# A fused attention and gated feed-forward kernel: batch 0 from a hand-written list, its bounds as pair tiles in two passes, two queues in written order, preparation shared differently between ACT and DVE

## The chip, the cores and the metric

The kernel runs on one core of one Trainium2 chip. Its engines are TensorE (PE), VectorE (DVE), ScalarE (ACT) and GpSimd (POOL); SyncE (SP) issues most of the DMA. The metric is the device time of one execution in microseconds (us), and where a kernel ran several times the median is quoted. The kernel before took 366.93 us (median of 3 runs, 365.98 to 369.07).

## The reference, cut to what matters

```python
# q, k, v: 4 batches x 8 heads x 768 rows x 64, fp32;  x: 3072 tokens x 512;  d_ff 1536
k_min, k_max = per chunk of 32 keys                      # 24 chunks
ub  = sum_d max(q * k_min, q * k_max)                    # upper bound of q.k in a chunk
ub  = where(causal by chunk, ub, -1e9)
sel = the 6 chunks with the largest ub, for each query
attn = softmax(where(sel and causal, q k^T / 8, -1e9))
x    = attn @ v, heads side by side
out  = (sigmoid(x @ w_gate) * (x @ w_val)) @ w_out
```

## The kernel before

The work goes in eight units of half a batch: 0a, 0b, 1a, ..., 3b. A unit has 384 queries; an "a" unit holds rows 0 to 383 of a batch, a "b" unit rows 384 to 767. A unit has three parts:

- **Preparation**: keys and queries are transposed on TensorE, two heads (a pair) to a block of PSUM, the memory in which this kernel's matmuls leave their results. From the keys come each chunk's maxima and minima, and an f16 copy `headK`. From the queries come their positive and negative parts (the "signs", `qs`) and an f16 copy `headQ`. A bounds matmul and a pick give 0/1 marks, written as 32 more rows under `headQ`. Under `headK` lies a fixed pattern (`epat`) that turns a mark into a large negative score.
- **Attention**: score matmuls, exp on ACT, a causal select on POOL, value matmuls.
- **FFN**: twelve gate and value blocks and three output blocks.

A loop merges the attention of unit i, the preparation of unit i+1 and the FFN of unit i-1. Inside that loop a scheduler may reorder the instructions of each engine. Only `first_prep` is held as written.

```python
def fill_kept(i, eng):                    # eng: gpsimd, for both buffers
    eng.memset(kcat[i], 0.0)
    eng.memset(v16s[i][:, :, :, D:D + 1], 1.0)
    for h in range(H):
        eng.tensor_copy(headK[i][64:96, h, :], epat)      # pattern under the keys

def keys_t(u, p, pool):                   # p: pair of heads
    ...                                   # 3 transposes into ps, 2 reduces on DVE into u.kmm
def keys_f(u, p, engs):
    ps = u.kps.pop(p)
    for e in range(2):
        engs[e](headK[u.b % 2][0:64, 2 * p + e, u.rows], ps[64 * e:64 * e + 64])

def chunks_t(u):                          # kmax over kmin, one head to 128 rows
    c0 = T // CH * u.half
    for e in range(2):
        for i in range(2):
            nc.scalar.copy(kcat[u.b % 2][64 * i:64 * i + 64, e:H:2, c0:c0 + T // CH],
                           u.kmm[64 * e:64 * e + 64, :, i, :])

def queries_t(u, p, pool):
    ...                                   # 3 transposes into ps
    for e in range(2):
        src = ps[64 * e:64 * e + 64]
        nc.scalar.activation(u.qs[0:64, 2 * p + e, s0:T], src[:, s0:T], AF.Relu)
        nc.vector.tensor_scalar_min(u.qs[64:128, 2 * p + e, s0:T], src[:, s0:T], 0.0)

def ffn_gv(u, fb):                        # one gate and one value block
    gp = pff.tile(...)                    # 4 matmuls
    nc.scalar.activation(gate, gp, AF.Tanh, scale=0.5)
    vp = pff.tile(...)                    # 4 matmuls; pff has 3 buffers
    nc.vector.scalar_tensor_tensor(hg, gate, 1.0, vp, ALU.add, ALU.mult)

SV = (nc.scalar.copy, nc.vector.tensor_copy)
SS = (nc.scalar.copy, nc.scalar.copy)
def prep_tasks(u):                        # for every unit but 0a
    r = [(0.0, lambda: regroup(u, "k", GP)), (0.0, lambda: regroup(u, "q", GP))]
    for p in range(NP):
        r.append((0.4, lambda p=p: (keys_t(u, p, ppr), keys_f(u, p, SV))))
    r.append((0.0, lambda: (chunks_t(u), cast_v(u))))
    for p in range(NP):
        r.append((0.4, lambda p=p: (queries_t(u, p, ppr), queries_f(u, p, SS))))
    ...                                   # bounds, pick, pick_t

load(units[1])
with tc.manual_schedule():                # this part runs as written
    fill_kept(0, nc.gpsimd)
    first_prep(units[0])
load_w(0)
...                                       # the loop that merges; fill_kept(1, nc.gpsimd) at i == 0
```

The softmax here doesn't subtract the row's maximum and nothing guards it: scores larger than these inputs give would overflow.

Of the kernel before, what the change touches and what calls it, by code (L numbers as in the profile page):

```python
# [18 lines left out]
def kernel(  # L19
# [10 lines left out]
    nc = tc.nc  # L30

# [28 lines left out]
    class Unit:  # L60
        def __init__(self, b, half):
            self.b, self.half = b, half
            self.name = f"{b}{'ab'[half]}"
            self.qa, self.qb = HB * half, HB * half + HB
            self.rows = slice(T * half, T * half + T)
            self.sel0 = 1 - half
            self.m = HB - self.sel0
            self.cb = T // CH * (half + 1)
            self.banks = HIGH if half else LOW
            self.where = {}  # L70
            base = 0
            for bk in self.banks:
                for (jb, i0, n) in bk:
                    for o in range(0, n, 128):
                        self.where[((i0 + o) // 128, jb)] = base + o
                    base += n
            self.width = base
            self.att, self.pv, self.kps, self.qps, self.ubT = {}, {}, {}, {}, {}
# [25 lines left out]
    def regroup(u, n, parts):  # L104
# [7 lines left out]
    load(units[0])  # L112

    ident32 = consts.tile([128, 128], F32, tag="id32")
    make_identity(nc, ident32)
    ident16 = consts.tile([128, 128], F16, tag="id16")
    nc.vector.tensor_copy(ident16, ident32)
    epat = consts.tile([32, NC, CH], F16, tag="epat")
    nc.vector.memset(epat, 0.0)
    nc.gpsimd.affine_select(  # L120
        out=epat, in_=epat, compare_op=ALU.not_equal, fill=NEG,
        base=0, pattern=[[-1, NC], [0, CH]], channel_multiplier=1,
    )
    epat = epat.rearrange("p c s -> p (c s)")
    NQ = 2 * HB - 1
    pen = consts.tile([128, NQ, NC], F32, tag="pen")
    nc.vector.memset(pen, 0.0)
    nc.gpsimd.affine_select(
        out=pen, in_=pen, compare_op=ALU.is_ge, fill=-1e9,
        base=128, pattern=[[128, NQ], [-CH, NC]], channel_multiplier=1,  # L130
    )

# [8 lines left out]
    def fill_kept(i, eng):  # L141
        eng.memset(kcat[i], 0.0)
        eng.memset(v16s[i][:, :, :, D:D + 1], 1.0)
        for h in range(H):
            eng.tensor_copy(headK[i][64:96, h, :], epat)  # L145

    nc.vector.memset(apt[0], 0.0)
    nc.vector.memset(apt[1], 0.0)
    nc.vector.memset(headQ[0][64:96, :, 0:128], 0.0)
# [8 lines left out]
    def load_w(i):  # L158
        lo, hi = 512 * i, 512 * i + 512
        tc.keep_in_program_order(nc.gpsimd.dma_start(wg16[:, :, lo:hi], wgs[:, :, lo:hi]))  # L160
        tc.keep_in_program_order(nc.gpsimd.dma_start(wv16[:, :, lo:hi], wvs[:, :, lo:hi]))

    def load_wo(i):
        tc.keep_in_program_order(nc.gpsimd.dma_start(wo16[:, 4 * i:4 * i + 4, :], wos[:, 4 * i:4 * i + 4, :]))
# [4 lines left out]
    def keys_t(u, p, pool):  # L169
        if p == 0:  # L170
            u.kmm = sel.tile([128, NP, 2, T // CH], F32, tag="kmm", name=f"kmm_{u.name}")
        ps = pool.tile([128, T], F32, tag="ps", name=f"kT_{u.name}_{p}")
        for x in range(HB):
            nc.tensor.transpose(ps[:, x:T:HB],  # L174
                                u.k[:, x, 2 * p:2 * p + 2, :].rearrange("p h d -> p (h d)"), ident32)
        pv = ps.rearrange("p (c s) -> p c s", s=CH)
        for e, op in enumerate((ALU.max, ALU.min)):
            nc.vector.tensor_reduce(out=u.kmm[:, p, e, :], in_=pv, op=op, axis=AX.X)  # L178
        u.kps[p] = ps

    def keys_f(u, p, engs):
        ps = u.kps.pop(p)
        for e in range(2):
            engs[e](headK[u.b % 2][0:64, 2 * p + e, u.rows], ps[64 * e:64 * e + 64])  # L184

    def chunks_t(u):
        c0 = T // CH * u.half
        for e in range(2):
            for i in range(2):
                nc.scalar.copy(kcat[u.b % 2][64 * i:64 * i + 64, e:H:2, c0:c0 + T // CH],  # L190
                               u.kmm[64 * e:64 * e + 64, :, i, :])

    def queries_t(u, p, pool):
        if p == 0:
            u.qs = sel.tile([128, H, T], F32, tag="qs", name=f"qs_{u.name}")
        ps = pool.tile([128, T], F32, tag="ps", name=f"qT_{u.name}_{p}")
        for x in range(HB):
            nc.tensor.transpose(ps[:, x:T:HB],  # L198
                                u.q[:, x, 2 * p:2 * p + 2, :].rearrange("p h d -> p (h d)"), ident32)
        s0 = 128 * u.sel0  # L200
        for e in range(2):
            src = ps[64 * e:64 * e + 64]
            nc.scalar.activation(u.qs[0:64, 2 * p + e, s0:T], src[:, s0:T], AF.Relu)
            nc.vector.tensor_scalar_min(u.qs[64:128, 2 * p + e, s0:T], src[:, s0:T], 0.0)
        u.qps[p] = ps

    def queries_f(u, p, engs):
        ps = u.qps.pop(p)
        for e in range(2):
            engs[e](headQ[u.half][0:64, 2 * p + e, :], ps[64 * e:64 * e + 64])  # L210

    def bounds(u, j):
        s0 = 128 * u.sel0
        n = T - s0
        ps = ppr.tile([128, T], F32, tag="ps", name=f"ubT_{u.name}_{j}")
        for i in range(4):
            nc.tensor.matmul(ps[32 * i:32 * i + 32, 0:n], kcat[u.b % 2][:, 4 * j + i, :],  # L217
                             u.qs[:, 4 * j + i, s0:T], start=True, stop=True)
        t = ubp.tile([128, T], F32, tag="ubT", name=f"ubTs_{u.name}_{j}")
        nc.scalar.copy(t[:, 0:n], ps[:, 0:n])  # L220
        u.ubT[j] = t
# [18 lines left out]
    def pick_t(u, j):  # L240
        ps = ppr.tile([128, T], F16, tag="ps", name=f"apT_{u.name}_{j}")
        for x in range(u.sel0, HB):
            nc.tensor.transpose(ps[:, 128 * x:128 * x + 128],  # L243
                                apt[j][:, x, :, :].rearrange("p h c -> p (h c)"), ident16)
        s0 = 128 * u.sel0
        for i in range(4):
            if i % 2 == 0:
                nc.scalar.copy(headQ[u.half][64:96, 4 * j + i, s0:T], ps[32 * i:32 * i + 32, s0:T])  # L248
            else:
                nc.vector.tensor_copy(headQ[u.half][64:96, 4 * j + i, s0:T], ps[32 * i:32 * i + 32, s0:T])  # L250

    def score(u, h, x):
# [5 lines left out]
        ps = psc.tile([128, n], F32, tag="ps", name=f"sc_{u.name}_{h}_{x}")  # L258
# [70 lines left out]
    VS = (nc.vector.tensor_copy, nc.scalar.copy)  # L329
    SV = (nc.scalar.copy, nc.vector.tensor_copy)  # L330
    SS = (nc.scalar.copy, nc.scalar.copy)
    GP = [(nc.gpsimd.tensor_copy, 0, H)]

    def prep_tasks(u):
        r = [(0.0, lambda: regroup(u, "k", GP)), (0.0, lambda: regroup(u, "q", GP))]
        for p in range(NP):
            r.append((0.4, lambda p=p: (keys_t(u, p, ppr), keys_f(u, p, SV))))
        r.append((0.0, lambda: (chunks_t(u), cast_v(u))))
        for p in range(NP):
            r.append((0.4, lambda p=p: (queries_t(u, p, ppr), queries_f(u, p, SS))))  # L340
# [4 lines left out]
        for j in range(2):  # L345
            r.append((0.06 * u.m, lambda j=j: pick_t(u, j)))
        return r

    def first_prep(u):
        A, V, G = nc.scalar.copy, nc.vector.tensor_copy, nc.gpsimd.tensor_copy  # L350
        regroup(u, "k", [(V, 0, 2), (A, 2, 4)])
        regroup(u, "k", [(V, 4, 6), (A, 6, 8)])
        for p in range(NP):
            keys_t(u, p, (ppr, ppr, psc, psc)[p])
            keys_f(u, p, SS)
        regroup(u, "q", [(A, 0, 2), (G, 2, 4), (A, 4, 6), (G, 6, 8)])
        for p in range(NP):
            queries_t(u, p, (psc, ppr, ppr, psc)[p])
            if p == 1:
                chunks_t(u)  # L360
                queries_f(u, 0, SS)
                queries_f(u, 1, SV)
                bounds(u, 0)
        cast_v(u)
        pick(u, 0)
        queries_f(u, 2, SS)
        bounds(u, 1)
        queries_f(u, 3, SS)
        pick_t(u, 0)
        pick(u, 1)  # L370
        pick_t(u, 1)
# [39 lines left out]
    load(units[1])  # L411
    with tc.manual_schedule():
        fill_kept(0, nc.gpsimd)
        first_prep(units[0])
    load_w(0)
    prev = []
    for i, u in enumerate(units):
        prep = []
        if i + 1 < len(units):
            prep = prep_tasks(units[i + 1])  # L420
# [3 lines left out]
        if i == 0:  # L424
            a.append((0.0, lambda: fill_kept(1, nc.gpsimd)))
            for n in range(3):
                a.insert(len(a) * (n + 1) // 4, (0.0, (lambda n=n: load_w(n + 1)) if n < 2 else (
                    lambda: [load_wo(j) for j in range(3)])))
# [34 lines left out]
```

## Time and profile before

| | before |
|---|---|
| time, median | 366.93 us |
| span of the profiled execution | 366.9 us (this run took 368.6, the slow end of the runs) |
| TensorE (PE) busy | 320.4 us, 87% |
| ACT, DVE, POOL busy | 67%, 56%, 24% |
| first score matmul of 0a, 0b, 1a | 19.8, 62.3, 107.6 us (of 0a one ran alone at 19.8; the others begin at 25.3, the figure in the prediction) |

The first lines of the page of before follow: the span, and the busy share of PE and POOL in 40 slices (one digit is tenths, one slice is 9.2 us). PEclk is the granted TensorE clock; its digits before a kernel's first clock record (39.9 us here) say nothing, as the durations below show.

```profile
span 366.9 us, 7168 instructions
...
PE   3353757999999899998999899999999899999996
...
POOL 9729832022132221122042201112011011110000
PEclk9999955699999999999999999999999999999999
```

PE is full from the eighth slice on and poorly used before. The table of stretches of before says the same in microseconds. Each line has a window, its length, then the busy time of PE, of its weight loads, of DVE, ACT and POOL, then the clock, the DMA share and GB/s. The stretches begin and end at the first score matmul of a unit: start to 0a, 0a to 0b, then 2a to 2b ("an a stretch": attention of 2a, preparation of 2b, FFN of 1b) and 2b to 3a ("a b stretch").

```profile
core 0: us, PE busy (x) PEld busy (x) DVE busy (x) ACT busy (x) POOL busy (x), PEclk, DMA share, GB/s
0.00:19.80 19.80, 7.67 (x34) 5.64 (x35) 9.54 (x22) 11.31 (x26) 15.62 (x28) 1.00 1.02 240
19.80:62.26 42.46, 24.27 (x171) 14.73 (x169) 23.59 (x87) 22.99 (x55) 23.53 (x28) 0.82 1.17 236
...
187.47:224.10 36.63, 34.60 (x291) 21.33 (x287) 26.48 (x76) 25.92 (x62) 9.86 (x12) 1.00 0.06 22
224.10:267.31 43.21, 41.07 (x399) 26.50 (x396) 24.07 (x68) 34.23 (x78) 7.09 (x10) 1.00 0.05 20
```

In the later stretches PE is idle for about 2 us of 36.6 and of 43.2. In the first 62 us PE is busy for only 32. Part of that loss is on POOL, in the timeline of before from 24 to 34 us (start, duration, engine, line, operation, output and input, and in brackets the idle time before it and what ended it):

```profile
26.53 1.47 POOL L167 CAST v_134<-v_0b 128x1536 f16<-128x1536 f32 x1 [5.27 <-DMA v_0b<-in_v_dram]
28.06 3.92 POOL L145 COPY hk_136<-epat 32x768 f16<-32x768 f16 x5
32.06 0.51 POOL L268 TENSOR_SCALAR_AFFINE_SELECT att_0a_318<-att_0a_318 128x384 f16<-128x384 f16 x1
```

POOL waits 5.3 us for the next unit's values, casts them, and copies the pattern of the second key buffer. Only then does it run the first causal select, although its input is ready at 26.4 us (the exp of 0.60 us from 25.81, in the timeline of ACT). The table of waits of before, from 20 to 40 us (who waits for whom: us in total, times, longest), shows the price on PE:

```profile
PE pv_0a_354 L282 <- POOL att_0a_318 L268: 5.8, 1, 5.8
```

PE is also slow. The query of one FFN block of before (durations min/median/max in ns, then first and last start) has a gate group in which the same 384-column matmul takes 326 or 526 ns:

```profile
L303 PE MATMUL g_0a_690<-xT_0a,wg_143 x4: 326/526/528, 43.3 to 65.6; 128*128 128x384 f16 x4
```

The Trainium skill ("TensorE: Matmul & The Clock Gate", Part 1) says that the array runs at half rate by default and is released by a window of about 3.4 us of sustained work. This trace agrees: PE was cold (half rate) to 39.9 us, warm (full rate) to 46.7, and cold again to 70.6. The first clock record is the switch at 39.9; that PE was cold before it shows in the 128x128 fp32 transposes, which took 417 to 421 ns at 5, 12 and 34 us and 273 to 291 in 2b's preparation. In the 3.41 us before the switch PE was busy for 3.10.

Here are PE's two longest waits of before between 187.47 and 224.1 us:

```profile
PE v_1b_2881 L309 <- ACT gate_1b_2843 L306: 1.2, 1, 1.2
PE xps_2a_2731 L295 <- DVE xnat_2a L288: 0.3, 1, 0.3
```

And here is ACT in the timeline of before, where it prepares 2b's queries, up to gate 2843, the only one that PE waited for in this stretch:

```profile
203.51 0.47 ACT L203 ACTIVATE qs_2b<-qT_2b_2828 64x384 f32<-64x384 f32 x1
203.88 0.95 ACT L210 CAST hq_137<-qT_2b_2796 64x384 f16<-64x384 f32 x2
204.74 0.49 ACT L203 ACTIVATE qs_2b<-qT_2b_2828 64x384 f32<-64x384 f32 x1
205.25 0.49 ACT L306 ACTIVATE gate_1b_2843<-g_1b_2838 128x384 f16<-128x384 f32 x1
```

This gate stands behind two sign operations and two query copies, 1.7 us of work. Other gates of the stretch follow a single sign operation (2811, for one, behind 0.48 us), and PE doesn't wait for them.

### The profile page before, as it was taken

The numbers are of one execution on the slowest core, as the hardware profiler recorded it, in microseconds if no ns is written. First come the engines' busy times: TensorE is split into PE (matmuls) and PEld (weight loads), VectorE is DVE, ScalarE is ACT, GpSimd is POOL, SyncE is SP. The second block draws the span as 40 slices with busy tenths as digits, with TensorE's granted clock in tenths as the row PEclk, the third lists the DMA queues.
The fourth block names the chain that finished last, engine by engine and source line by source line (L and its number), as shares of the span: only waits on it lengthen the run. The fifth ranks groups of instructions, "written<-read, shape, count | busy, mean of one in ns | idle before, by whom it ended". The sixth has DMA issues, their size and how long they took to land.

```text
span 366.9 us, 7168 instructions
## 1 busy us (share of the span) xinstructions
PE 320.4 (87%) x2704; PEld 201.2 (55%) x2704; DVE 204.5 (56%) x581; ACT 247.5 (67%) x560; POOL 88.5 (24%) x125
## 2 busy tenths in 40 slices
PE   3353757999999899998999899999999899999996
PEld 2133524666456546675566546665566456665652
DVE  6343865586259747675258746863468664432430
ACT  4763753779666975789576948698567948764331
POOL 9729832022132221122042201112011011110000
PEclk9999955699999999999999999999999999999999
DMA  8999999920319222031210001000100010001002
GB/s 222 265 245 272 226 200 236 223 63 29 116 60 172 88 86 88 0 88 29 88 59 2 0 30 59 2 2 0 59 30 1 2 58 30 2 0 59 29 2 86
DMA packets 50098, 30.34 MB, mean 83 GB/s; under 512 B 26000, under 2 KB 46992, under 8 KB 50064
## 3 DMA queue, kind: packets, MB, share of 16 engines
q1 hardware_dynamic: 45312, 25.17, 25.8%
q0 software_dynamic: 4752, 4.72, 7.6%
q8 instruction: 21, 0.34, 0.4%
q14 instruction: 13, 0.11, 0.1%
HBM read 28.31 MB, written 6.29 MB: 94 GB/s over the span
## 4 chain that ended last, share of the span: by engine, by line
PE 60%; ACT 19%; DVE 8%; SPq 4%; DMA 3%; issue 3%; POOL 2%; ACTq 0%; POOLq 0%
DMA v_0b<-in_v_dram 3%; SPq L102 3%; ACT hq_137 L210 2%; ACT hq_132 L210 2%; SPq L96 1%; POOL hk_136 L145 1%; DVE hk_131 L184 1%; DVE hk_136 L184 1%; PE o_2b_4223 L318 1%; PE o_1b_2995 L318 1%; PE o_0b_1757 L318 1%; PE o_3a_4827 L318 1%; PE o_2a_3709 L318 1%; PE o_0a_1233 L318 1%; PE o_1a_2471 L318 1%
## 5 line engine op out<-in xcount | busy, mean ns | idle before, releaser
L309 PEld LDWEIGHTS <-wv_144 128*128 128x128 f16 x384 | 37.7, 98 | 29.5 <-issue 5.8
L303 PEld LDWEIGHTS <-wg_143 128*128 128x128 f16 x384 | 34.9, 99 | 15.5 <-issue 2.6
L262 PEld LDWEIGHTS <-hk_131 96*128 96x128 f16 x240 | 21.2, 106 | 11.0 <-issue 6.0
L262 PEld LDWEIGHTS <-hk_136 96*128 96x128 f16 x240 | 19.2, 97 | 9.1 <-issue 2.6
L145 POOL COPY hk_136<-epat 32x768 f16<-32x768 f16 x8 | 6.4, 822 | 0.3
L145 POOL COPY hk_131<-epat 32x768 f16<-32x768 f16 x8 | 6.4, 845 | 0.1
L282 PE MATMUL pv_0a_354<-v_134,att_0a_318 128*128 128x65 f16 x6 | 0.5, 243 | 5.8 <-POOL att_0a_318 L268 5.8
L174 PE MATMUL kT_0a_174<-ident_113,k_0a 128*128 128x128 f32 x3 | 0.9, 430 | 5.1 <-DVE k_0a L110 5.1
L265 ACT ACTIVATE att_0a_369<-sc_0a_0_370 128x512 f16<-128x512 f32 x1 | 0.6, 597 | 5.6 <-PE sc_0a_0_370 L262 5.6
L198 PE MATMUL qT_0a_212<-ident_113,q_0a 128*128 128x128 f32 x3 | 0.9, 440 | 4.0 <-ACT q_0a L110 4.0
L178 DVE TENSOR_REDUCE kmm_0b<-kT_0b_342 128x12 f32<-128x384 f32 x2 | 1.1, 558 | 5.7 <-PE kT_0b_342 L174 5.7
L282 PEld LDWEIGHTS <-att_0a_318 128*128 128x128 f16 x6 | 0.4, 126 | 6.4 <-POOL att_0a_318 L268 6.4
L248 ACT COPY hq_137<-apT_0b_632 32x384 f16<-32x384 f16 x2 | 0.9, 468 | 4.3 <-PE apT_0b_632 L243 4.2
L217 PE MATMUL ubT_0a_236<-qs_0a,kcat_130 128*32 128x256 f32 x8 | 1.6, 634 | 2.4 <-ACT kcat_130 L190 2.4
L295 PEld LDWEIGHTS <-xnat_0a 128*128 128x128 f16 x12 | 1.2, 118 | 4.2 <-issue 4.2
L174 PEld LDWEIGHTS kT_0a_174<-ident_113,k_0a 128*128 128x128 f32 x3 | 0.5, 213 | 5.1 <-issue 5.1
L217 PE MATMUL ubT_0a_277<-qs_0a,kcat_130 128*32 128x256 f32 x8 | 1.1, 631 | 2.3 <-DVE ubm_0a_263 L231 2.3
L286 DVE RECIPROCAL rz_0b_1206<-pv_0b_1111 128x6 f32<-128x6 f32 x1 | 0.2, 196 | 5.2 <-PE pv_0b_1111 L282 5.2
L286 DVE RECIPROCAL rz_1b_2444<-pv_1b_2349 128x6 f32<-128x6 f32 x1 | 0.2, 196 | 5.2 <-PE pv_1b_2349 L282 5.2
L286 DVE RECIPROCAL rz_2b_3682<-pv_2b_3587 128x6 f32<-128x6 f32 x1 | 0.2, 195 | 5.2 <-PE pv_2b_3587 L282 5.2
L110 ACT COPY k_0a<-rawk_0a 128x384 f32<-128x384 f32 x2 | 1.0, 512 | 2.9 <-DMA rawk_0a<-in_k_dram 2.9
L243 PEld LDWEIGHTS <-ap_138 128*128 128x128 f16 x20 | 2.0, 111 | 1.6
(2039 smaller groups left out, 1105.9 us busy)
## 6 DMA issues: line engine op xcount, KB each, us to landing
wg_143<-in_moe_w_gate_dram POOLq DMA_DIRECT2D x3, 512.0 KB, 8.0
wv_144<-in_moe_w_val_dram POOLq DMA_DIRECT2D x3, 512.0 KB, 10.6
wo_145<-in_moe_w_out_dram POOLq DMA_DIRECT2D x3, 512.0 KB, 18.8
rawk_0a<-in_k_dram SPq DMA_DIRECT2D x2, 384.0 KB, 3.8
rawq_0a<-in_q_dram SPq DMA_DIRECT2D x2, 384.0 KB, 5.9
v_0a<-in_v_dram SPq DMA_DIRECT2D x3, 256.0 KB, 6.9
rawk_0b<-in_k_dram SPq DMA_DIRECT2D x2, 384.0 KB, 5.0
rawq_0b<-in_q_dram SPq DMA_DIRECT2D x2, 384.0 KB, 6.8
```

The costliest lines, as they stand in the source:

```text
L96: nc.sync.dma_start(t[:, 4 * j:4 * j + 4], src[u.b, 4 * j:4 * j + 4, u.rows].rearrange("h (p x) d -> p h x d", x=HB))
L102: nc.sync.dma_start(u.v[:, i], v[u.b, :, r:r + 128].rearrange("h p d -> p h d"))
L145: eng.tensor_copy(headK[i][64:96, h, :], epat)
L174: nc.tensor.transpose(ps[:, x:T:HB], u.k[:, x, 2 * p:2 * p + 2, :].rearrange("p h d -> p (h d)"), ident32)
L184: engs[e](headK[u.b % 2][0:64, 2 * p + e, u.rows], ps[64 * e:64 * e + 64])
L210: engs[e](headQ[u.half][0:64, 2 * p + e, :], ps[64 * e:64 * e + 64])
L217: nc.tensor.matmul(ps[32 * i:32 * i + 32, 0:n], kcat[u.b % 2][:, 4 * j + i, :], u.qs[:, 4 * j + i, s0:T], start=True, stop=True)
L243: nc.tensor.transpose(ps[:, 128 * x:128 * x + 128], apt[j][:, x, :, :].rearrange("p h c -> p (h c)"), ident16)
L262: nc.tensor.matmul(ps[:, o:o + w], headK[u.b % 2][:, h, 128 * jb:128 * jb + 128], headQ[u.half][:, h, i:i + w], start=True, stop=True)
L303: nc.tensor.matmul(gp, wg16[:, c, 128 * fb:128 * fb + 128], u.xT[:, c, :], start=(c == 0), stop=(c == 3))
L309: nc.tensor.matmul(vp, wv16[:, c, 128 * fb:128 * fb + 128], u.xT[:, c, :], start=(c == 0), stop=(c == 3))
L318: nc.tensor.matmul(op, hgl[(u.name, fc)][:, 128 * tb:128 * tb + 128], wo16[:, fc, :], start=(fc == 0), stop=(fc == NFB - 1))
```

## The change

The change wants to shorten the beginning. There are five parts.

1. Preparation and attention of 0a, preparation of 0b, and nine of 0a's twelve gate-and-value blocks come from one hand-written list for all engines (`opening`). 0b's preparation moves under 0a's FFN.
2. POOL and the DMA queue of SyncE run in written order for the whole kernel, not only in the opening.
3. The pattern under the keys is written by two DMAs, no longer by 16 copies on POOL.
4. In batch 0 the bounds are computed on pair tiles: max(q,0) against the maxima, then min(q,0) against the minima, the second pass accumulating on the first. Maxima and minima then stay where the reduce left them, and the operations that stack them (`kcat`) drop out there.
5. For batches 1 to 3 the work of preparation is shared differently between ACT and DVE. All signs of a pair go to one engine, and so do all its key copies. In "b" units three pairs of signs and all key copies go to ACT; in "a" units two pairs of signs go to ACT and all key copies to DVE. The `kcat` operations move from ACT to DVE (eight instead of four). Query copies, all on ACT before, alternate between ACT and DVE by pair, the copies of one block of marks all go to one engine, and q is regrouped two pairs later.

```diff
+    ctx.enter_context(tc.manual_schedule(engines={nc.gpsimd.engine, nc.sync.engine}))
...
+            self.paired = b == 0
...
-        for h in range(H):
-            eng.tensor_copy(headK[i][64:96, h, :], epat)
+    def fill_pattern(i, eng):                                   # eng: sync
+        eng.dma_start(headK[i][64:96],
+                      epat.rearrange("p c s -> p (c s)").unsqueeze(1).to_broadcast([32, H, S]))
...
+    def chunks_t(u, j):
+        c0 = T // CH * u.half
+        for e in range(2):
+            for i, sign in enumerate((1.0, -1.0)):
+                nc.vector.tensor_scalar_mul(kcat[...], u.kmm[...], sign)
...
+    def signs(u, p, eng):
...
+        for e in range(2):
+            src = u.qps[p][64 * e:64 * e + 64, s0:T]
+            for i, sign in enumerate((1.0, -1.0)):
+                o = u.qs[64 * i:64 * i + 64, 2 * p + e, s0:T]
+                if eng is A:
+                    nc.scalar.activation(o, src, AF.Relu, scale=sign)
+                elif i == 0:
+                    nc.vector.tensor_scalar_max(o, src, 0.0)
+                else:
+                    nc.vector.tensor_scalar(o, src, -1.0, 0.0, ALU.mult, ALU.max)
...
     def bounds(u, j):
-        for i in range(4):
+        for i, e in [(i, e) for e in range(2) for i in range(4)] if u.paired else []:
+            h, r = 4 * j + i, 64 * (i % 2)
+            nc.tensor.matmul(ps[32 * i:32 * i + 32, 0:n], kmx[r:r + 64, h // 2, e, :],
+                             u.qs[r:r + 64, h - h % 2 + e, s0:T], start=(e == 0), stop=(e == 1))
+        for i in [] if u.paired else range(4):
...
     def prep_tasks(u):
-        r = [(0.0, lambda: regroup(u, "k", GP)), (0.0, lambda: regroup(u, "q", GP))]
+        even = [A, V, A, V] if u.half == 0 else [A, A, A, V]
+        kf = [V, V, V, V] if u.half == 0 else [A, A, A, A]
+        qf = [A, V, A, V]
+        r = [(0.0, lambda: regroup(u, "k", [(G, 0, H)]))]
         for p in range(NP):
-            r.append((0.4, lambda p=p: (keys_t(u, p, ppr), keys_f(u, p, SV))))
+            if p == 2:
+                r.append((0.0, lambda: regroup(u, "q", [(G, 0, H)])))
+            r.append((0.4, lambda p=p: (keys_t(u, p, ppr), extremes(u, p), keys_f(u, p, kf[p]))))
...
-    def first_prep(u):
...
+    def opening(u, w):                    # u = 0a, w = 0b: some 120 calls in written order
+        load(u); constants(); load(w)     # (joined here)
...
+        bounds(u, 0)
...
+        score(u, 0, 0)
+        score(u, 0, 1, pff, "ff")
...
+        more()                            # one gate-and-value block of 0a's FFN
+        keys_t(w, 2, ppr)
+        extremes(w, 2)
+        keys_f(w, 2, A)
+        more()
...
+        signs(w, 0, V)
+        queries_f(w, 0, A)
...
```

## The prediction

> **What bounds the kernel now.** Two regimes. From about 75 us to the end TensorE is the limit: the table of stretches gives it 37.8 to 38.2 us busy in every 40 us between 115 and 315, ACT 29.5 to 30.6, DVE 23 to 28. At most 2 us of each 40 are idle. The first 70 us hold only 39 us of PE busy, mostly at half speed. The timeline shows why. (a) POOL copies the pattern into the kept keys (16 copies of 0.82 us) and casts v_0b, for which it waits 5.3 us, ahead of the first causal select; PE stands from 26.7 to 32.6 (the wait table: 5.8 us on att_0a). (b) The first q regroup starts at 9.6 because POOL was copying until then. (c) The preparation of 0b ping-pongs between ACT and DVE from 43 to 62 so PE turns slow: 384-column matmuls last 526 ns there, 326 later. The Trainium skill ("TensorE: Matmul & The Clock Gate", Part 1) says that the array starts at half rate until about 3.4 us of sustained work; the trace agrees: fast from 40 to 45.6, slow again to 71. (d) The FFN of 0a really starts after 65, with its fourth transposed piece.
>
> **What the change does.** Removes 13 us of POOL copies (two DMAs instead) and the early v_0b wait; takes four kcat copies (0.95 us on ACT) out of batch 0's chain; adds a second pass of bounds matmuls there (estimate: 1.6 us becomes about 3 cold). Moves 0b's preparation from under attention to under the FFN of 0a. For later units, ACT loses about 5 us per "a" preparation (kcat, keys, half of the queries), DVE gains as much ("b": about even); each pair's signs sit on one engine.
>
> **Sum, from durations of the trace.** q landed at about 7.7, regrouped 8.5, first bounds 11 to 14, first mask 17 to 19, second bounds to 23, first score about 24 (25.3 before, but with no stall after). Eight heads at 1 us of ACT plus query and key copies: attention 0a and its turns end at about 37 (65 before). Then nine FFN steps (9 x 1.3), transposes, bounds and picks: about 18 us of warm PE against 14 ACT and 16 DVE; with bubbles 20, so 0b's scores start at about 57 with nine FFN steps done. The old kernel had about 4.5 steps and 2.3 heads done at 75: in PE work the new one is 3 us further at 57. Gain 21. The attention of 0b then has only 12 us of FFN beside it and is ACT and PE bound (28 each): lose 2. Steady state is 95% PE: gain 0 to 3, say 1. Nearly all of this is on the critical path: everything later is PE bound.
>
> Predicted time: **347 us**, 80% range 339 to 356. Chances: faster by over 2% 0.94, within 2% 0.05, slower 0.01.
>
> **Right or wrong would show as**: no POOL wait for v_0b ahead of the first select; first FFN matmul at 34 to 40; fast matmuls (326 ns) from about 30 on; first 0b score at 54 to 60; first output-projection matmul (93.5 before) near 70; a 40 us stretch in the steady part still 37.5 to 38.5 PE; FFN tail unchanged (about 23 us).
>
> **What would make it wrong**: three score buffers shared with values and queries stall the hand-written list; weights land late; PE stays cold through the FFN phase (plus 8); written order on POOL or the DMA queue delays selects or loads later; the lighter ACT fills PE's last idle (down to 340).

## The result

The kernel after took 356.20 us (median of 4 runs, 355.64 to 356.60), against 367.01 in the same rounds. The ratio is 0.9698 with a 95% interval of 0.9653 to 0.9743. Ratios here are the mean time of one kernel's runs over that of the other's of the same rounds, so they are not quite the ratio of the medians that are quoted. The gain by medians is 10.8 us, where 20 was predicted; 356.2 lies 0.2 us above the upper end of the range.

The profiled executions differ by more, 366.9 - 353.9 = 13.0 us. The profiled run of before was 1.6 us above its median, and that of after 0.6 us below. The sums below are of the two traces.

The page of after, the same lines:

```profile
span 353.9 us, 7200 instructions
...
PE   4678687999988999999987999999998999999995
...
POOL 3393204211420040210421032201421011110000
PEclk9979999999999999999999999999999999999999
```

The stretches of after, with the columns of before, again from one unit's first score matmul to the next: start to 0a, 0a to 0b, 0b to 1a, then 2a to 2b and 2b to 3a:

```profile
0.00:15.84 15.84, 8.35 (x60) 5.14 (x61) 10.29 (x35) 7.85 (x16) 6.31 (x14) 1.00 0.99 237
15.84:55.67 39.83, 29.55 (x243) 19.02 (x242) 24.05 (x78) 23.20 (x53) 13.34 (x18) 0.91 1.18 223
55.67:87.51 31.84, 29.95 (x317) 19.66 (x315) 25.59 (x83) 25.54 (x55) 8.39 (x11) 1.00 0.34 93
169.16:208.30 39.14, 35.75 (x290) 21.57 (x287) 26.43 (x80) 27.63 (x62) 8.39 (x11) 1.00 0.31 82
208.30:250.95 42.65, 40.76 (x399) 26.36 (x395) 29.36 (x85) 30.77 (x66) 8.39 (x11) 1.00 0.29 75
```

The opening is better, as intended. The a stretch is longer, 39.1 us against 36.6, and the b stretch shorter, 42.65 against 43.2. The times at which the units' first scores start, read from the two timelines, make the account:

| first score of | before | after | lead of after |
|---|---|---|---|
| 0a | 19.8 | 15.8 | 4.0 |
| 0b | 62.3 | 55.7 | 6.6 |
| 1a | 107.6 | 87.5 | 20.1 |
| 1b | 144.3 | 126.5 | 17.7 |
| 2a | 187.5 | 169.2 | 18.3 |
| 2b | 224.1 | 208.3 | 15.8 |
| 3a | 267.3 | 251.0 | 16.3 |
| 3b | 303.9 | 290.1 | 13.8 |
| end | 366.9 | 353.9 | 13.0 |

Twenty microseconds are won by the start of 1a. By then the two kernels are at the same point of the work (2154 matmuls are left in before, 2157 in after), so the lead is real and on the critical path. After that each a stretch gives back about 2.5 us, each b stretch returns 0.6, and the tail loses 0.8. That is -7.5 + 1.1 - 0.8, or about -7.

The opening's gain shows on POOL, in the timeline of after. The first select now comes before the wait for v_0b:

```profile
18.42 0.56 POOL L295 TENSOR_SCALAR_AFFINE_SELECT att_0a_279<-att_0a_279 128x384 f16<-128x384 f16 x1 [3.40 <-ACT att_0a_279 L292]
...
34.23 1.47 POOL L169 CAST v_114<-v_0b 128x1536 f16<-128x1536 f32 x1 [6.12 <-DMA v_0b<-in_v_dram]
```

POOL waits even longer for v_0b than before, 6.1 us, but nothing urgent stands behind the cast. The clock records of after show PE warm from 7.8 to 21.5 us and again from 28.3 on, in place of 70.6. The states that both traces show from end to end lasted 6.83 and 23.89 us in before and 13.65 and 6.83 in after, which is 2, 7, 4 and 2 times 3.41 us, as the skill's window would have it.

Part of what happens in the a stretch is shown by PE's waits of after between 169.16 and 208.3 us. They answer to those of before in 187.47 to 224.1:

```profile
PE v_1b_2839 L336 <- ACT gate_1b_2805 L333: 1.1, 1, 1.1
PE ubT_2b_2953 L247 <- ACT hq_117 L236: 0.7, 1, 0.7
PE v_1b_2875 L336 <- ACT gate_1b_2837 L333: 0.7, 1, 0.7
PE xps_2a_2721 L322 <- DVE xnat_2a L315: 0.6, 1, 0.6
```

And here is ACT in the timeline of after, at the same work as the four lines of before:

```profile
182.95 1.96 ACT L227 ACTIVATE qs_2b<-qT_2b_2790 64x384 f32<-64x384 f32 x4
184.92 0.96 ACT L236 CAST hq_117<-qT_2b_2790 64x384 f16<-64x384 f32 x2
185.90 0.49 ACT L333 ACTIVATE gate_1b_2805<-g_1b_2800 128x384 f16<-128x384 f32 x1
...
186.77 1.97 ACT L227 ACTIVATE qs_2b<-qT_2b_2822 64x384 f32<-64x384 f32 x4
188.76 0.49 ACT L333 ACTIVATE gate_1b_2837<-g_1b_2832 128x384 f16<-128x384 f32 x1
```

The first gate stands behind four sign operations and two query copies, 2.9 us of work in one piece, and the second behind four more sign operations, on an engine that has time to spare (27.63 us busy in 39.14). The Trainium skill ("TensorE: Matmul & The Clock Gate", Part 1, on engine queue depths) calls ACT's and DVE's queues strict FIFO. The trace is in line with that: the two gates that PE waits for by name, 2805 and 2837, are the two behind these blocks.

These waits are only a part of the 2.5 us, and before had its own. PE's waits for gates grew from 1.2 to 1.8 us, its wait for query copies ahead of the bounds from 0.2 to 0.7, and all its idle time in the stretch by 1.4 (from 36.63 - 34.60 to 39.14 - 35.75). The other 1.15 us are in PE's busy time, for practically the same matmuls (291 and 290). Of these, 0.8 lie in the first group of bounds matmuls: ubT_2b_2953 shows 1.7 us for eight, with a value block between the second and the third, where before shows 0.9. So waits behind ACT's blocks are seen, but more than half of the loss isn't traced to them.

### The profile page after: what moved, and what is told of

It is laid out like the page before. It is cut to its first block, busy times and chain, and to the rows that moved or that the text cites. A ratio compares the mean times of both kernels' runs of the same rounds, so it can differ in the third digit from the quotient of the medians.

```text
span 353.9 us, 7200 instructions
## 1 busy us (share of the span) xinstructions
PE 316.5 (89%) x2736; PEld 197.0 (56%) x2736; DVE 216.4 (61%) x642; ACT 234.4 (66%) x501; POOL 74.1 (21%) x106
## 4 chain that ended last, share of the span: by engine, by line
PE 54%; ACT 16%; issue 10%; DVE 8%; DMA 5%; SPq 4%; POOL 2%; ACTq 0%; POOLq 0%; DVEq 0%
DMA v_0b<-in_v_dram 5%; SPq L104 2%; ACT hq_117 L236 2%; SPq L98 1%; ACT hq_112 L236 1%; ACT qs_2b L227 1%; ACT qs_3b L227 1%; ACT qs_1b L227 1%; ACT hk_116 L198 1%; PE o_2b_4225 L345 1%; PE o_1b_2989 L345 1%; PE o_1a_2399 L345 1%; ACT qs_1a L227 1%; PE o_2a_3645 L345 1%; PE o_0b_1743 L345 1%
## 5 line engine op out<-in xcount | busy, mean ns | idle before, releaser
L336 PEld LDWEIGHTS <-wv_121 128*128 128x128 f16 x384 | 37.0, 97 | 38.4 <-issue 16.6
L330 PEld LDWEIGHTS <-wg_120 128*128 128x128 f16 x384 | 35.2, 98 | 16.1 <-issue 1.9
L289 PEld LDWEIGHTS <-hk_111 96*128 96x128 f16 x240 | 19.7, 101 | 13.0 <-issue 8.2
L289 PEld LDWEIGHTS <-hk_116 96*128 96x128 f16 x240 | 19.2, 97 | 9.4 <-issue 3.1
L277 ACT COPY hq_117<-apT_0b_735 32x384 f16<-32x384 f16 x4 | 1.9, 469 | 1.8 <-PE apT_0b_735 L273 1.8
L192 DVE TENSOR_SCALAR kcat_110<-kmm_2b 64x24 f32<-64x24 f32 x8 | 2.8, 350 | 0.1
L192 DVE TENSOR_SCALAR kcat_115<-kmm_3b 64x24 f32<-64x24 f32 x8 | 2.8, 350 | 0.1
L277 DVE COPY hq_112<-apT_3a_3801 32x256 f16<-32x256 f16 x4 | 1.2, 288 | 2.7 <-PE apT_3a_3801 L273 2.7
L277 DVE COPY hq_112<-apT_2a_2555 32x256 f16<-32x256 f16 x4 | 1.2, 288 | 2.7 <-PE apT_2a_2555 L273 2.7
L169 POOL CAST v_114<-v_0b 128x1536 f16<-128x1536 f32 x1 | 1.5, 1465 | 6.1 <-DMA v_0b<-in_v_dram 6.1
L273 PEld LDWEIGHTS <-ap_118 128*128 128x128 f16 x20 | 1.7, 98 | 1.5 <-DVE ap_118 L267 0.2
L162 POOL DMA_DIRECT2D wg_120<-in_moe_w_gate_dram x3 | 2.4, 808 | 0.0
L198 ACT CAST hk_111<-kT_0b_494 64x384 f16<-64x384 f32 x2 | 0.9, 474 | 2.2 <-DVE kmx L186 2.2
L169 POOL CAST v_114<-v_0a 128x1536 f16<-128x1536 f32 x1 | 1.5, 1469 | 4.4 <-DMA v_0a<-in_v_dram 4.4
```

Of the source, the lines that this page charges most:

```text
L169: nc.gpsimd.tensor_copy(v16s[u.b % 2][:, u.qa:u.qb, :, 0:D], u.v)
L192: nc.vector.tensor_scalar_mul(kcat[u.b % 2][64 * i:64 * i + 64, 4 * j + e:4 * j + 4:2, c0:c0 + T // CH], u.kmm[64 * e:64 * e + 64, 2 * j:2 ...
L198: eng(headK[u.b % 2][0:64, 2 * p + e, u.rows], ps[64 * e:64 * e + 64])
L277: eng(headQ[u.half][64:96, 4 * j + i, s0:T], ps[32 * i:32 * i + 32, s0:T])
L289: nc.tensor.matmul(ps[:, o:o + w], headK[u.b % 2][:, h, 128 * jb:128 * jb + 128], headQ[u.half][:, h, i:i + w], start=True, stop=True)
L330: nc.tensor.matmul(gp, wg16[:, c, 128 * fb:128 * fb + 128], u.xT[:, c, :], start=(c == 0), stop=(c == 3))
```

## The experiments

The main theory was that the new split of work between ACT and DVE lengthens the a stretch, because whole pairs of signs and all key copies sit on ACT's in-order queue in front of the gates. The rival was that written order on POOL and the DMA queue does, by holding back selects or loads. Both came with the change. Twelve kernels were run. The outputs are right. All edits are against the kernel after unless said otherwise. The table gives all of them; a stretches are 1a to 1b, 2a to 2b and 3a to 3b.

| run | median us | ratio to before (95%) | first score 0a, 0b, 1a | a stretches | b stretch |
|---|---|---|---|---|---|
| before | 366.93 | | 19.8, 62.3, 107.6 | 36.6 each | 43.2 |
| after | 356.20 | 0.9698 (0.9653 to 0.9743) | 15.8, 55.7, 87.5 | 39.0, 39.2, 39.2 | 42.6 |
| e1_split_b | 352.96 | 0.9620 (0.9583 to 0.9657) | 16.7, 56.7, 88.6 | 38.7, 37.7, 37.7 | 42.6 |
| e2_old_prep | 350.56 | 0.9576 (0.9512 to 0.9639) | 16.3, 56.2, 88.9 | 36.8, 36.6, 36.6 | 43.2 |
| e3_free_order | 364.29 | 0.9926 (0.9885 to 0.9967) | 17.7, 57.3, 96.9 | 40.1, 38.8, 38.8 | 42.1 |
| e4_before_written | 363.38 | 0.9904 (0.9867 to 0.9940) | 19.8, 57.9, 103.3 | 36.6 each | 43.2 |
| e5_before_newprep | 371.56 | 1.0113 (1.0073 to 1.0152) | 20.5, 61.6, 105.2 | 38.8 each | 42.1 |
| e6_evac_first | 352.34 | 0.9589 (0.9553 to 0.9626) | 16.1, 51.6, 83.4 | 39.0 to 39.2 | 42.7 |
| e7_one_pass | 366.38 | 0.9974 (0.9933 to 1.0016) | 21.6, 66.7, 98.5 | 39.0 to 39.2 | 42.6 |
| e8_best_mix | 344.36 | 0.9381 (0.9335 to 0.9427) | 16.2, 51.7, 83.5 | 37.2, 36.6, 36.6 | 42.7 |
| e9_evac_prep | 355.03 | 0.9661 (0.9610 to 0.9712) | 20.0, 60.0, 91.9 (late start) | 38.5, 38.2, 38.2 | 42.4 |
| e10_pool_copies | 360.69 | 0.9809 (0.9775 to 0.9844) | 20.7, 60.9, 92.8 | as after | as after |
| e11_best_evac | 344.21 | 0.9368 (0.9335 to 0.9400) | 16.2, 52.4, 84.3 | 37.2, 36.6, 36.6 | 42.4 |
| e12_split_evac | 353.19 | 0.9621 (0.9590 to 0.9652) | 16.8, 56.8, 88.7 | 38.8, 37.7, 37.7 | 42.4 |

The rounds had their own runs of before, with medians from 366.88 to 367.71 us. Kernels of different rounds are compared through their ratios and through their traces.

### e1_split_b: the b units split as the a units are

```diff
-        even = [A, V, A, V] if u.half == 0 else [A, A, A, V]
-        kf = [V, V, V, V] if u.half == 0 else [A, A, A, A]
+        even = [A, V, A, V]
+        kf = [V, V, V, V]
```

> The changed kernel, with one difference: the preparation of every second half batch from batch 1 on uses the engine split of the first halves (keys all on DVE, signs ACT, DVE, ACT, DVE instead of keys all on ACT and signs ACT, ACT, ACT, DVE). Theory 1 (the new split puts blocks of up to 3 us of preparation on ACT's in-order queue, gates wait behind them and PE behind the gates): the stretches from the first score of an 'a' half to the first score of the next 'b' half, 39.1 us in the changed kernel and 36.6 before, fall by 1 to 3 us each; total 348 to 352 us against 356. Theory 2 (written order on POOL and the DMA queue makes them long): no change, 355 to 357.

The a stretch, in which the b unit is prepared, fell from 39.2 to 37.7 us, and the b stretch stayed at 42.6. The line of the table of stretches of e1 for 2a to 2b:

```profile
169.83:207.50 37.67, 35.30 (x290) 21.28 (x287) 30.84 (x92) 22.78 (x50) 8.40 (x11) 1.00 0.32 85
```

ACT has 4.85 us less to do than in the kernel after (22.78 against 27.63), DVE 4.4 us more (30.84 against 26.43), and PE is done 1.5 us earlier. PE no longer waits for a gate by name. So what this split puts on ACT is a large part of the loss. The run does not separate the load itself from who waits for whom: with the keys on DVE, both readers of a key block are also on one engine. It isn't all of the loss, since the stretch of before was 36.6. PE's longest wait is now 0.87 us, before the gate matmuls at 187.61, for a product on DVE (187.00) that stands behind two key copies and seven `kcat` operations, 2.4 us of work. The blocks have in part moved to DVE.

### e2_old_prep: the old preparation for batches 1 to 3, everything else as after

```diff
-    r.append((0.4, lambda p=p: (keys_t(u, p, ppr), extremes(u, p), keys_f(u, p, kf[p]))))
+    r.append((0.4, lambda p=p: (keys_t(u, p, ppr), extremes(u, p), keys_f2(u, p, SV))))
-    r.append((0.0, lambda: (chunks_t(u, 0), chunks_t(u, 1), cast_v(u))))
+    r.append((0.0, lambda: (chunks_t2(u), cast_v(u))))          # four copies on ACT, as before
-    ... signs(u, p, even[p]), queries_f(u, p, qf[p]) ...
+    ... signs2(u, p), queries_f2(u, p, SS) ...                  # positive part ACT, negative part DVE
```

> The changed kernel with the preparation of all half batches from batch 1 on as the old kernel wrote it (engines, order, and both regroups at its start); opening and written order as changed. Theory 1 (the split): the 'a' stretches return to 36.6 to 37.2 us and the 'b' stretches to about 43.2 from 42.65, total 348 to 351. Theory 2 (written order): 355 to 357. Theory 3 (it is the order that the scheduler happens to give PE): anything, with the 'a' stretches not near 36.6.

The a stretches are back at 36.6 us (36.8 the first) and the b stretches at 43.2, both as before. The line of e2 for 2a to 2b:

```profile
168.88:205.46 36.58, 34.77 (x291) 21.23 (x288) 26.36 (x76) 25.92 (x62) 8.35 (x11) 1.00 0.32 87
```

The opening and the written order are those of the kernel after, and the loss is gone. Without the new preparation the a stretches are not long. It is also what makes the b stretches 0.6 us shorter. This kernel is 5.6 us faster than the kernel after by medians; by ratios it is 0.9576 against 0.9698.

### e3_free_order: no written order on POOL and the DMA queue after the opening

```diff
-    ctx.enter_context(tc.manual_schedule(engines={nc.gpsimd.engine, nc.sync.engine}))
```

> The changed kernel without the line that keeps POOL and the DMA queue in written order for the whole program (the opening stays a hand-written list on all engines). Theory 1 (the split): 'a' stretches still 38.5 to 39.5 us, total 354 to 358. Theory 2 (written order): 'a' stretches back to about 36.6, total 348 to 351.

It got 8 us slower, nearly all of it between 0b and 1a (39.6 us in place of 31.8). The a stretches hardly moved: 38.8 in batches 2 and 3. As the main cause of the long a stretches, the rival is refuted, and over the whole kernel written order gains time. The timeline of POOL in e3 shows what the scheduler did with its freedom:

```profile
57.70 1.47 POOL L168 CAST v<-v_1a 128x1536 f16<-128x1536 f32 x1 [19.66 <-DMA v_1a<-in_v_dram]
...
65.86 1.47 POOL L168 CAST v<-v_1b 128x1536 f16<-128x1536 f32 x1 [5.05 <-DMA v_1b<-in_v_dram]
67.29 0.99 POOL L294 TENSOR_SCALAR_AFFINE_SELECT att_0b<-att_0b 128x384 f16<-128x384 f16 x2
```

Two casts that wait for loads stand ahead of 0b's first select. PE stands from 61.9 to 67.9 us; its next value matmuls show a wait of 5.98 us for that select. This is the same fault as (a) of the prediction, one unit later.

### e4_before_written: the kernel before, with that one line added

```diff
     nc = tc.nc
+    ctx.enter_context(tc.manual_schedule(engines={nc.gpsimd.engine, nc.sync.engine}))
```

> The old kernel with only that line added: POOL and the DMA queue in written order throughout. Theory A (most of the 20 us by which the new opening leads comes from the hand-written list, which also moves 0b's preparation and the FFN): the 5.8 us stall on POOL goes because the cast of the second half's v no longer comes ahead of the first select, but the weights are loaded only as far as POOL gets; total 360 to 366. Theory B (most of the gain is POOL's order): total 350 to 358. Theory 2 predicts longer 'a' stretches, near 39; theory 1 leaves them at 36.6.

The 5.8 us wait of PE on att_0a is gone; PE's longest wait between 19 and 58 us is 2.3, and POOL casts v_0b at 32.8, after the first select at 26.5. 0b starts 4.4 us earlier and all later stretches are as before. The time is 3.5 us lower than before's in the same rounds, 1.0%, and the interval lies wholly below 1. Reading (a) of the prediction, that POOL's order costs the old kernel several microseconds, is shown, though the line orders the DMA queue too and no run separates the two. Of the 5.8 us that PE stood, 3.5 (medians) to 4.5 (traces) come through to the end.

### e5_before_newprep: the kernel before, with the new preparation for batches 1 to 3

```diff
-            prep = prep_tasks(units[i + 1])
+            prep = (new_prep_tasks if i > 0 else prep_tasks)(units[i + 1])
```

> The old kernel with one part of the change: the preparation of the half batches from batch 1 on as the new kernel writes it (engines and place of the second regroup). Theory 1 (this split costs the steady part what the opening won): 'a' stretches go from 36.6 to 38.5 to 39.5 us, 'b' stretches from 43.2 to about 42.4, total 370 to 375 against 367. If the split costs only together with the new opening: 365 to 368.

The a stretches grew from 36.6 to 38.8 us and the b stretches shrank from 43.2 to 42.1. The time is 1.1% longer than before. The new preparation loses by itself, without the opening and without written order. With e2 this settles from both sides that the new preparation is the cause, as a whole. Written order has a small share: e3 and e5, with the new preparation but without written order, both show 38.8 and 42.1 us, after 39.15 and 42.65. With the new preparation it thus costs about 0.35 us of an a stretch and 0.55 of a b stretch; with the old one (e2 and e4 against before) nothing.

### e6_evac_first: in the opening's FFN phase the copy for the attention reads the block first

In the kernel after, a PSUM block of keys is read by DVE (maxima, minima) and then by ACT (the copy to `headK`); queries likewise. No data pass between the two readers, yet ACT's copy waits for DVE. The Trainium skill ("PSUM — Partial Sum Buffer", "PSUM bank collisions raise a hardware error") gives a possible reason: the compiler's back end makes any two instructions of different engines on the same bank and group of 32 partitions depend on each other, reads included. The records don't say what placed the dependency in this kernel. The timeline of after shows what follows from it:

```profile
36.03 0.49 ACT L333 ACTIVATE gate_0a_539<-g_0a_534 128x384 f16<-128x384 f32 x1
36.56 0.55 DVE L339 SCALAR_TENSOR_TENSOR hg_0a_546<-gate_0a_539,v_0a_541 128x384 f16<-128x384 f16 x1 [1.59 <-ACT gate_0a_539 L333]
...
37.03 1.01 DVE L186 TENSOR_REDUCE kmx<-kT_0b_548 128x12 f32<-128x384 f32 x2
...
38.13 0.96 ACT L198 CAST hk_111<-kT_0b_548 64x384 f16<-64x384 f32 x2 [1.61 <-DVE kmx L186]
39.12 0.49 ACT L333 ACTIVATE gate_0a_566<-g_0a_561 128x384 f16<-128x384 f32 x1
```

It is a ring: gate (ACT), product (DVE, behind the gate), reduces (DVE, behind the product), key copy (ACT, behind the reduces), next gate (ACT, behind the copy). One turn takes 3.1 us. The edit turns the last dependency between the engines around:

```diff
         keys_t(w, 2, ppr)
-        extremes(w, 2)
         keys_f(w, 2, A)
+        extremes(w, 2)
 # the same for pair 3, and queries_f(w, p, A) ahead of signs(w, p, V) for pairs 0, 1 and 3
```

> The changed kernel; in the opening's FFN phase alone the ACT copies out of each transposed block come ahead of the DVE operations on the same block, where the list had them after (the order on every engine stays the same, only who waits for whom over a PSUM block turns round). Theory R (a ring: gate on ACT, product on DVE, extremes on DVE, key copy on ACT, next gate, 3.0 us a round where PE has 1.6 us of work): the ring opens, the first score of 0b comes at 51 to 53.5 us against 55.7, total 352 to 354.5 against 356. Rival (the phase is held by the landing of weights or of v, or by DVE's own load): first score of 0b at 55 to 56, total 356.

The order of instructions on each engine is the same; only who waits for whom has changed. The timeline of e6:

```profile
34.77 0.49 ACT L333 ACTIVATE gate_0a<-g_0a 128x384 f16<-128x384 f32 x1
35.16 0.95 ACT L198 CAST hk<-kT_0b 64x384 f16<-64x384 f32 x2
...
36.13 0.49 ACT L333 ACTIVATE gate_0a<-g_0a 128x384 f16<-128x384 f32 x1
36.18 1.02 DVE L186 TENSOR_REDUCE kmx<-kT_0b 128x12 f32<-128x384 f32 x2
```

Gates now follow each other after 1.4 us here, and after 1.6 us in the rounds that follow. ACT's waits for DVE's signs between 30 and 56 us fell from 5.3 to 0.6 us, and those for the reduces from 3.8 to 2.2. 0b starts 4.1 us earlier and the whole kernel is 3.9 us faster by medians.

### e7_one_pass: batch 0's bounds stacked in one pass, as in the other batches

```diff
-            self.paired = b == 0
+            self.paired = False
 # opening: chunks_t(u, 0) ahead of bounds(u, 0), chunks_t(u, 1) after extremes(u, 3),
 #          chunks_t(w, 0) after extremes(w, 1), chunks_t(w, 1) after extremes(w, 3)
```

> The changed kernel with batch 0's bounds in one pass as in the other batches (kcat filled by eight small DVE operations per pair of pairs, 0.35 us each, signs of 64 partitions in four operations a pair). If the paired form in two passes pays in the opening: first score of 0a at 19 to 22 us against 15.8, and the first score of 0b 4 to 8 us later than 55.7, total 359 to 365. If it does not: 355 to 357.

It took 10.2 us longer by medians, and 11.1 in the traces. 5.8 us are lost by 0a's first score, 11.0 by 0b's, and nothing later. The first bounds start at 11.5 us, behind a 2.3 us wait for `kcat`, where after has them at 8.7. In that order PE also ran at half clock until about 34 us, and again from 51 to 55. So this is the price of the stacking in this list and not of the operations alone: the list was written for pair tiles and wasn't tuned again.

### e10_pool_copies: the pattern copied by POOL, as before

```diff
     def fill_pattern(i, eng):
-        eng.dma_start(headK[i][64:96], ...)
+        for h in range(H):
+            nc.gpsimd.tensor_copy(headK[i][64:96, h, :], epat.rearrange("p c s -> p (c s)"))
```

> The changed kernel, with the mask pattern put into the kept keys by eight POOL copies of 0.82 us per buffer, as the old kernel did, in place of a DMA. If the DMA is what frees POOL for the first regroup of q: first transposes of q at about 10.5 to 12 us against 7.6, first score of 0a 2.5 to 4.5 us later than 15.8, total 358.5 to 361. If POOL's time there is free: 355.5 to 357.

It took 4.5 us longer by medians. The eight copies of the first buffer occupy POOL from 2.45 us on for 6.33 us. The regroup of q, which the first query transposes need, then starts at 9.25 (6.7 in after), and 0a's first score at 20.7 us in place of 15.8. The later stretches are as in the kernel after. Reading (b) is shown.

### e8_best_mix: e6, and the old split for the b units alone

From e2 and e6 together: the b units (prepared in the a stretches) get the old split back, with the new sign convention, and the a units keep the new one, because it shortens the b stretches.

```diff
-        prep = prep_tasks(units[i + 1]) if i + 1 < len(units) else []
+        prep = (prep_tasks_b if (i + 1) % 2 else prep_tasks)(units[i + 1]) if i + 1 < len(units) else []
 # prep_tasks_b: as in e2, with Relu of -q and -kmin; and the turn of e6
```

> A kernel meant to beat both: the change, with the turned-round copies of the opening's FFN phase, and with the second halves from batch 1 on prepared in the old kernel's split (the new sign convention kept), the first halves in the new one. If the parts add up: 'a' stretches 36.6 to 37, 'b' stretches 42.6 to 43, 0b starts at 51 to 53.5, total 344 to 349. If the scheduler answers each mix with another order: 'a' stretches 37 to 39, total 349 to 354.

344.36 us, 6.2% below before and 11.8 us below the kernel after by medians. The two gains add: 4.0 us by the start of 1a, 6.8 in the three a stretches, 0.6 in the tail and 0.1 lost in the b stretches make 11.3, the difference of the two traces. It beats both kernels.

### e9_evac_prep, e11_best_evac and e12_split_evac: the turn of e6 in the later preparations

These ask whether the remedy of e6 also cures the long a stretches.

```diff
 # e9: after, with this in prep_tasks
-    (keys_t(u, p, ppr), extremes(u, p), keys_f(u, p, kf[p]))
+    (keys_t(u, p, ppr), keys_f(u, p, kf[p], False), extremes(u, p))
-    (queries_t(u, p, ppr), signs(u, p, even[p]), queries_f(u, p, qf[p]))
+    (queries_t(u, p, ppr), queries_f(u, p, qf[p], False), signs(u, p, even[p]))
 # e11: e8 with the same turn in the a units' preparation;  e12: e1 with the same turn
```

> The changed kernel with the copies out of each transposed block written ahead of the DVE reductions and signs on it, in the preparation of all half batches from batch 1 on (the opening is left as changed, the engine split too). Theory R in the steady part (what costs the 'a' stretches 2.5 us is ACT's key copies waiting for DVE's extremes, as in the opening's ring): 'a' stretches 36.6 to 38, total 349 to 353. Theory L (it is the load itself: blocks of signs, 1.96 us each, and of key copies on ACT ahead of gates): 'a' stretches 38.7 to 39.5, total 355 to 357.

> The best kernel so far (344.4 us) with the turned-round copies in the preparation of its first halves as well. Theory R: 'b' stretches fall from 42.7 by 0.2 to 0.8 us each, total 342.5 to 344. Theory L: same, 344 to 345.

> The changed kernel with both repairs of the steady part at once: the second halves' preparation in the split of the first halves (alone: 'a' stretches 37.7 us) and the copies out of each block ahead of the DVE work on it (alone: 38.2 to 38.5). If ACT's load and the turn over each block are the whole 2.5 us and add up: 'a' stretches 36.6 to 37.1, total 350 to 352. If they remedy the same waits: 37.5 to 37.8, total 352 to 353.5. If a third cause (small kcat operations on DVE, 2.8 us a half) holds the rest: 37.2 to 37.7.

e9's a stretches fell to 38.2 us, which is 1.0 of the 2.5 lost. That isn't cleanly the turn's doing. In the kernel after one of the eight `kcat` operations of 2b lasted 1.40 us, beside POOL's cast of v_2b (181.8 to 183.3 us), where their median is 0.175; in e9 none of 2b's runs beside the cast and the longest lasts 0.47 (beside a select of 0.52 on POOL), so DVE, too, was freed of about a microsecond. What that is worth to PE, no run shows. Its four runs fell into two groups, 352.8 and 353.4, and 356.7 and 357.2, so its median says little. The profile fell in the late group: the first half of q landed later (the regroup of q at 8.6 us against 6.7) and PE was warm for good only from 31.9 us, against 28.3, both before the part that was edited.

e11 equals e8 within the noise. e12 equals e1: its a stretches are 37.7 us, too. Neither could show more. In the split of the a units every block has both its readers on one engine (keys all on DVE; signs and query copies of a pair both on ACT or both on DVE), so there is no wait between engines for the turn to reverse. Whether the turn and a lighter ACT would add in a split that has such waits was not tested. The 1.1 us between 37.7 and the old 36.6 stay open. Candidates are the eight `kcat` operations on DVE (1.4 us for each b unit in e1 and e12, and in front of the product for which PE waits 0.9), written order (0.35, from e3 and e5) and the order that the scheduler gives PE. No run separates them; e2 and e8 only go around the question.

## Why the prediction was right or wrong

**Right: what bounded the kernel before.** None of the four readings of the first 70 us was contradicted. (a) is shown by e4, (b) by e10. Readings (c) and (d) were seen in the traces, and the measured lead at 1a agrees with them, though no run isolates them: fast matmuls come from 28.3 us on (predicted "from about 30"), and the FFN of 0a starts at 30.4, earlier than the predicted 34 to 40, in place of really after 65.

**Right: the gain of the opening.** The sum said 21 - 2 = 19 us by the end of 0b's attention. The traces show 20.1 at the first score of 1a (by their places among their fellows the two profiled runs may flatter this by up to 2.2). 0b's first score came at 55.7 (predicted 57) and the first output projection at 68.1 (predicted near 70). That the sum came out so close is partly luck, as two errors inside it cancelled:

- 0a's first score came at 15.8, not 24. The sum had a cold PE for the two-pass bounds and a late q. PE was warm from 7.8 us, and the bounds of the first four heads ran from 8.7 to 10.6.
- The FFN phase with 0b's preparation took 25.3 us (30.4 to 55.7), not 20. The ring between ACT and DVE made each turn 3.1 us. e6 gives back 4.1 us of it. The prediction added up engine times (18 of PE, 14 of ACT, 16 of DVE) and put 2 us on top for bubbles. Engine totals don't show a ring of waits.

**Wrong: the step "Steady state is 95% PE: gain 0 to 3, say 1".** It lost about 7 us. The three a stretches lost 7.5, the two b stretches gained 1.1, and the tail lost 0.8. This term is off by 8, and the opening gave 1.1 more than the sum's 19; together they make the 13.0 of the traces out of the predicted 20. The remaining 2.2 to the 10.8 of the medians are the places of the two profiled runs among their fellows.

The diff had been read as "ACT loses about 5 us per 'a' preparation, DVE gains as much ('b': about even)". As totals that is nearly right: in the stretch that prepares 2b, ACT went from 25.92 to 27.63 us and DVE from 26.48 to 26.43; in the one that prepares 3a, ACT fell by 3.5 and DVE rose by 5.3. But a stretch in which PE is 95% busy has no room for late work. The new split puts all four sign operations of a pair in one piece on ACT; gates stand behind it, and PE's next value matmul behind the gate. e2 takes the new preparation out and gets 36.6 us back, e5 puts it alone into the old kernel and gets 38.8. How the loss divides is shown only in part: PE's named waits for gates grew by just 0.6 us; e1, with the lighter ACT, recovers 1.5 of 2.5 us, and 1.1 stay open.

**Listed as risks.** "Written order delays selects or loads later" was the wrong way round. The written order is worth 8 us in the new kernel (e3) and 3.5 in the old (e4), and the prediction gave it no term of its own. "Weights land late" and "PE stays cold through the FFN phase" did not come about. The shared score buffers stalled the list little: from 15.8 to 30.4 us PE waited 1.1, 0.4 and 0.4 us for an exp ahead of a score. "The lighter ACT fills PE's last idle" came about only in the b stretches, with 0.6 us each.

**The 40 us stretches of PE.** The steady part was to show 37.5 to 38.5 us of PE in each 40. It showed 36.25 to 39.35. The FFN tail is unchanged, as predicted: from 3b's last transpose to the end 27.3 us in before and 27.6 in after. A table by units tells more, as an a stretch and a b stretch have different limits.

## What to carry to other kernels

Where one engine is 95% busy, do not judge a redistribution among the others by their totals: find what that engine waits for next, and count the longest piece of work that can stand in front of it in an in-order queue. When two engines read the same PSUM block, put first the reader whose queue holds the urgent work, because the other reader's wait is then the harmless one. Keep loads that may be late out of an in-order queue ahead of urgent small operations, and try a mixed kernel when a change helps one kind of stretch and hurts another.

## What the Trainium skill lacked or had wrong

- "PSUM — Partial Sum Buffer" ("PSUM bank collisions raise a hardware error") gives a reason why two readers of one block wait for each other. It doesn't say that the order of the readers can be worth much: with the same order on every engine, turning this wait around took 0b's start from 55.7 to 51.6 us and the kernel from 356.2 to 352.3 (e6).
- The same section lets different groups of 32 partitions of a bank be read at once. In the kernel before, DVE's copies of its 32-partition pieces of a marks block still waited for ACT's copies of other pieces, 12 times and 7.0 us in all for the a units. The runs don't tell whether that wait goes by block or by the tile that both write.
- "TensorE: Matmul & The Clock Gate", Part 4, says that transposes do not engage the full clock. In the kernel after only transposes ran on PE before 8 us, and the 128x128 fp32 transposes went from 421 ns (keys, at 4.9 us) to 272 ns (queries, at 8.1 us) while the clock record turned warm at 7.8. Whether these transposes use the transpose mode that the page means, the records do not say.
- The same page, Part 1, calls the ramp a penalty below 1% of a typical kernel's span. The kernel before was at half rate to 39.9 us and from 46.7 to 70.6, out of 366.9: some 64 us in all, in which a 384-column matmul took 526 ns instead of 326. PE was busy for about 36 of the 64 us; what the half rate cost in time no run measures.
- No page gives a way to see a ring of waits across two in-order queues. Here the sums of busy time (23.2 us of ACT and 24.1 of DVE in 39.8) did not show one whose opening in e6 gave 4.1 us.
